# Input transposed by the DMA instead of TensorE, with other activation tables, another parameter layout and another order, in a kernel of windowed attention and a long convolution

## The chip, the cores and the metric

The kernel runs on one core of a Trainium2 chip. The core has TensorE (PE; its weight loads are listed apart as PEld), VectorE (DVE), ScalarE (ACT), GpSimd (POOL) and SyncE (SP), and 16 DMA engines. SP, ACT and POOL issue DMAs from queues of their own, and each engine works through its own instructions in order. The metric is the device time of one execution in microseconds (us).

## The reference

Two branches read the same input `x` of 2048 tokens by 640 channels (bf16), and a gate mixes them. The convolution branch is given `x` as its input, and the separate input `B_u` is not used.

```python
g = sigmoid((x * gate_w).sum(-1, keepdims=True))
# a: attention, 32 heads of 20 channels; token s sees s, s-2, ..., s-14
q, k, v = split(x @ wqkv)
a = (softmax(q . k_window * 20 ** -0.5) . v_window) @ wo
# b: per channel d a kernel of 2048 taps from 192 complex exponentials
dt = exp(log_dt)
K[d, l] = real(sum_n C[d, n] * dt[d] * B[d, n] * exp(dt[d] * A[d, n] * l))
b = irfft(rfft(pad(x)) * rfft(pad(K))) + x * Dskip      # causal convolution
out = g * a + (1 - g) * b
```

`wqkv` is 640 by 1920, `wo` 640 by 640, and each of the six parameter arrays `A_re`, `A_im`, `B_re`, `B_im`, `C_re`, `C_im` is 640 by 192.

## The kernel before, in words

**The work and how it is ordered.** Nearly all work is written as tasks (class `Task`), which are collected in two plans, `"main"` and `"tail"`. A task names the engines that may run it, a planned duration, its dependencies, and at times a due time `rdy` before which a planner did not place it. The table `ORDER` holds, for each plan, the finished sequence: every entry is a step from one task to the next, and a letter behind it chooses the engine of a task that may run on ACT or DVE (the first engine named, ACT, where there is no letter). `emit` writes the instructions in that sequence and ties each instruction to the one before it on its engine, so each engine's order is fixed. What waits for what is settled on the chip by semaphores.

**Start.** `SSMParams.build` issues the loads from three queues. SP loads C_re, C_im, the first quarter of `x`, A_im, the second quarter, the three 640-column parts of `wqkv`, A_re and the other two quarters of `x`. ACT loads B_re, B_im, `log_dt`, `gate_w` and an identity matrix. `x` arrives in the tile `xn` with tokens on the partitions. The projections need channels on the partitions, so `window` (L192) plans ten tasks `turn`, each of eight 128x128 matmuls against the identity (L207) into a PSUM tile `ar`, and ten evictions (`tev`) that copy 128x1024 elements to `xT`, which lies in the buffer `bufA`.

**Projections.** `plan_late` computes q, k and v for four chunks of 512 tokens: 60 tiles `tb` of 128x512, five matmuls each (L291). The 60 evictions go to `pv` (first chunk) or `prj` (the others), by ACT at L473 or DVE at L475, which are the lines of the helper `evict`. From there POOL stores them to DRAM (`qS`, `kS`, `vS`), and `plan_core` reads them back in chunks of 256 tokens (`qc`, `kc`, `vc`). `plan_gate` computes the gate with 80 small matmuls on `xT` (L222).

**Attention.** For each of eight chunks DVE forms products of q with shifted k (`prod`, L345), PE sums them to logits (`lg`, L351), ACT takes the exponential, DVE normalises. SP stores the weights to DRAM (`aS`) and spreads them back (`asb`), DVE multiplies by v (`pv`, L415), PE sums (L422) and projects by `wo` (L446), and ACT or DVE scales by the gate (`ga`).

**Kernel taps.** From the parameters DVE and ACT make ten bf16 tables, called pieces (`pc`): phase digits, log magnitudes, an arctangent for the angle of C times B. That is one long chain of 128x960 instructions with Ln, Exp and Arctan. SP stores each piece into the DRAM table `Sprm` (L620), which has 640 channels, ten pieces and 192 numbers per channel. For each of ten groups of eight channels (`NCH` = 10), `load_L` (L724) loads the rows of that group into one of two tiles `L`. PE multiplies `L` by constants to arguments (`ar`, L767), ACT takes Sin (L782) and Exp (L784) of them into the buffers `big` and `bufA`, DVE multiplies these (`pt` L804, `qq` L806), PE sums over the 192 terms (`kps`, L822). The results `E` of five groups together are expanded (`KExpand`) and written to DRAM.

**Transform.** `first` transforms the taps (`f1`, `fk`) and the input (`fu`) by 128x256 matmuls (L1266; L1285 where a tile is split) with evictions of 128x1024 to `bufA` and `big`. `fft_conv` is the plan `"tail"`: forward transforms (`fp`, L1039) with evictions `sp_u` and `sp_k`, products on DVE (`ta`, `tc`, `Y`), inverse transforms (`cp`, `yp`), the mix with the attention branch (`tt`, `ot`), and the output's stores.

**Activation tables.** [...]

Of the kernel before, what the change touches and what calls it, by code (L numbers as in the profile page):

```python
# [20 lines left out]
S = 2048  # L21
# [17 lines left out]
def _attn_consts():  # L39
# [129 lines left out]
class Attn:  # L169
# [22 lines left out]
    def window(self, pl, cst, pa):  # L192
# [7 lines left out]
        for n in range(2 * NKT):  # L200
# [8 lines left out]
            def ev(en, hf=hf, kt=kt, b=b):  # L209
                evict(nc, en, self.xT[:, hf, kt, :], b["tx"][:].rearrange("p a b -> p (a b)"))  # L210
# [323 lines left out]
class SSMParams:  # L534
# [5 lines left out]
    def build(self, ctx, tc, pl, A_re, A_im, B_re, B_im, C_re, C_im, log_dt, gate_w, at_, pa, xl, wl):  # L540
# [19 lines left out]
        for w_ in wl:  # L560
            w_()
# [803 lines left out]
```

## Time and profile before

| | us |
|---|---|
| runs: median of 3 (lowest to highest) | 342.84 (342.28 to 346.0) |
| profiled execution: span from first to last instruction | 339.6 |
| busy PE / DVE / ACT in that span | 289.5 / 298.9 / 290.2 |
| first projection matmul (L291) starts | 16.44 |
| first Sin (L782) starts | 56.80 |
| first forward transform of the tail (`fp`) starts | 271.65 |

The profiled execution has no device time of its own beside its span. The span of 339.6 is 3.2 us under the median of the timed runs, and I take these 3.2 us as what lies around the span. The profile's rows give the start in us, the duration, the engine, the line, the operation, output and inputs, how often it was repeated (x...), and in brackets how long the engine sat idle and what released it. `SPq`, `ACTq` are the issuing of DMAs by that engine. In tables of stages the columns are the stretch, its length, then busy time and number of instructions of PE, PEld, DVE, ACT and POOL, the granted PE clock (1.00 is full), the mean busy share of the DMA engines and what they moved in GB/s.

### The profile page before, as it was taken

To read this page: it belongs to the slowest core of one execution; us is meant where nothing else is said; L and a number is where in the kernel's file an instruction comes from. 1 tells how busy PE (TensorE), PEld (TensorE's weight loads), DVE (VectorE), ACT (ScalarE), POOL (GpSimd) and SP (SyncE) were. 2 spreads that over 40 slices of the span, in tenths; PEclk is the share of its full clock that TensorE was granted. 3 is DMA by queue.
4 is the path that set the end of the run, shared out by engine and by line. 5 is a ranking of instruction groups with operands and counts; after the bars stand their busy time and mean duration, and the time that the engine had idled before them with its cause. 6 is when DMAs were issued, how large, how long until landed. Compare 5 with 4: busy or idle time off the path is not lost. (4 is left out here: it accounts for less than half of the span.)

```text
span 339.6 us, 12013 instructions
## 1 busy us (share of the span) xinstructions
PE 289.5 (85%) x5181; PEld 172.1 (51%) x5214; DVE 298.9 (88%) x407; ACT 290.2 (85%) x424; POOL 92.3 (27%) x119
## 2 busy tenths in 40 slices
PE   0699999999997899999999979669999899996760
PEld 0446544444453455455545444445765676665750
DVE  3999988789998799999899989786888979999982
ACT  1899737999997899999999998786976779998991
POOL 8603334041052161102137615621130000000053
PEclk9999999999998999999999999997999999999996
DMA  7997854378279781285738585982882336576056
GB/s 251 356 259 233 222 131 133 103 207 166 66 195 249 186 204 38 42 233 161 252 58 206 124 224 129 207 187 50 235 281 93 124 113 198 139 142 118 2 136 177
DMA packets 48949, 56.30 MB, mean 166 GB/s; under 512 B 25498, under 2 KB 40154, under 8 KB 48898
## 3 DMA queue, kind: packets, MB, share of 16 engines
q1 hardware_dynamic: 39928, 27.90, 31.2%
q0 software_dynamic: 8224, 27.04, 30.2%
q8 instruction: 40, 0.66, 0.8%
q10 hardware_dynamic: 746, 0.61, 0.5%
q14 instruction: 11, 0.09, 0.1%
HBM read 36.26 MB, written 19.27 MB: 164 GB/s over the span
## 5 line engine op out<-in xcount | busy, mean ns | idle before, releaser
L291 PE MATMUL tb<-bufA 128*128 128x512 bf16 x267 | 73.3, 389 | 5.0 <-issue 3.1
L782 ACT ACTIVATE big<-ar 128x740 bf16<-128x740 int16 (+1 forms) x72 | 56.1, 854 | 2.5 <-issue 1.2
L784 ACT ACTIVATE big<-ar 128x848 bf16<-128x848 f32 x60 | 50.3, 918 | 1.8 <-PE ar L767 1.8
L767 PE MATMUL ar<-Rarg,L 64*128 64x212 bf16 (+4 forms) x600 | 48.8, 253 | 3.5 <-ACT big L784 1.5
L345 DVE TENSOR_TENSOR prod<-qc,kc 128x2048 bf16<-128x2048 bf16 x40 | 47.8, 1218 | 4.2 <-PE lg L351 3.3
L415 DVE TENSOR_TENSOR pv<-vc,asb 128x2048 bf16<-128x2048 bf16 x40 | 48.2, 1217 | 0.9 <-PE tb L422 0.9
L291 PEld LDWEIGHTS <-bufA 128*128 128x128 bf16 x300 | 31.0, 122 | 28.0 <-issue 11.3
L822 PEld LDWEIGHTS <-pt 128*32 128x32 bf16 (+1 forms) x2560 | 25.8, 92 | 37.0 <-issue 34.4
L822 PE MATMUL kps<-qq,pt 128*32 128x21 bf16 (+1 forms) x2560 | 36.9, 173 | 8.0 <-issue 6.6
L804 DVE TENSOR_TENSOR pt<-big 128x1024 bf16<-128x1024 bf16 x48 | 33.3, 701 | 5.6 <-issue 2.0
L767 PEld LDWEIGHTS <-L 64*128 64x128 bf16 x600 | 20.6, 94 | 27.1 <-issue 23.4
L446 PE MATMUL tb<-wo_sb,oT 128*128 128x320 bf16 x160 | 28.6, 301 | 0.7 <-DVE ga L457 0.4
L1157 POOL DMA_DIRECT2D out_dram<-ot x14 | 7.7, 557 | 77.9 <-DVE ot L1139 77.9
L473 ACT ACTIVATE prj<-tb 128x512 bf16<-128x512 f32 x32 | 20.0, 632 | 8.8 <-PE tb L291 8.6
L422 PE MATMUL tb<-pv,ind 128*64 128x512 bf16 (+1 forms) x192 | 25.0, 363 | 2.5 <-issue 2.3
L473 ACT ACTIVATE sp_u<-fp 128x640 bf16<-128x640 f32 x31 | 23.9, 952 | 0.8 <-PE fp L1039 0.8
L473 ACT ACTIVATE sp_k<-fp 128x640 bf16<-128x640 f32 x29 | 22.6, 969 | 1.2 <-DMA PHX<-c_phi 1.0
L969 POOL COPY pace<-Usb 32x2 bf16<-32x2 bf16 x7 | 14.3, 2045 | 25.9 <-DMA Usb<-in_A_x_dram 25.9
L806 DVE TENSOR_TENSOR qq<-big 128x1344 bf16<-128x1344 bf16 x24 | 21.2, 883 | 0.0
L339 POOL DMA_DIRECT2D vc<-vS x16 | 11.9, 771 | 28.9 <-DVE pv L415 12.4
L1039 PEld LDWEIGHTS <-PHI 128*128 128x128 bf16 x160 | 15.5, 97 | 8.0 <-issue 1.0
L455 ACT ACTIVATE ga<-tb,g_sb 128x320 bf16<-128x320 f32 x26 | 13.8, 544 | 4.4 <-PE tb L446 3.0
(168 smaller groups left out, 562.4 us busy)
## 6 DMA issues: line engine op xcount, KB each, us to landing
vc<-vS POOLq DMA_DIRECT2D x16, 327.5 KB, 6.9
kc<-kS POOLq DMA_DIRECT2D x8, 337.5 KB, 6.1
xn<-in_A_x_dram SPq DMA_DIRECT2D x4, 640.0 KB
qc<-qS POOLq DMA_DIRECT2D x8, 320.0 KB, 5.9
gaS<-ga SPq DMA_DIRECT2D x8, 320.0 KB
Usb<-in_A_x_dram POOLq DMA_DIRECT2D x8, 320.0 KB, 5.1
gaF<-gaS SPq DMA_DIRECT2D x8, 320.0 KB
bufA<-in_A_wqkv_dram SPq DMA_DIRECT2D x3, 800.0 KB
```

The source lines that it names most:

```text
L291: nc.tensor.matmul(ppf, self.wq[:, which, kt, e::5], self.xT[:, c0 // 1024, kt, c0 % 1024:c0 % 1024 + SC], start=(kt == 0), stop=(kt == NK ...
L345: nc.vector.tensor_tensor(b[e][:], b["qc"][:, e, :].unsqueeze(1).to_broadcast([128, W, C]), win(b["kc"][:, e, :], 0, W, DIL, C), ALU.mult)
L415: nc.vector.tensor_tensor(o, vw, b["asb"][:].unsqueeze(2).to_broadcast(sh), ALU.mult)
L422: nc.tensor.matmul(b["op", e][64 * a:64 * a + 64, 0:n, :], ind[:, 32:96], b["pv", e][:, w, a, 0:n, :], start=(w == 0), stop=(w == 3), skip ...
L446: nc.tensor.matmul(apf[:, :320], b["oT"][:, e, i * 128:(i + 1) * 128], wo_sb[:, e, hf * 320:(hf + 1) * 320], start=(e == 0), stop=(e == 4))
L473: nc.scalar.activation(o, i, ACT.Identity)
L767: nc.tensor.matmul(ar[:, g2, a0:a0 + ncol], L[rows, sb, gv, l0:l0 + 128], R[rows, c0:c0 + ncol], start=True, stop=True, tile_position=(64 ...
L782: nc.scalar.activation(d_[:, :, s0 * QW:s1 * QW], ar[:].bitcast(I16)[:, :, 0:2 * (s1 - s0) * QW:2], ACT.Sin, scale=SCL)
L784: nc.scalar.activation(dst[:, gp::2].rearrange("p g s n -> p g (s n)"), ar[:, :, 0:2 * EW], ACT.Exp)
L804: nc.vector.tensor_tensor(pt[:, :, k, :], gg[:, :, ::-1] if k else gg, e1, ALU.mult)
L806: nc.vector.tensor_tensor(qq[:], trg[:, :, KI:].rearrange("p a (v m) -> p a v m", v=2), exq[:, :, KI:].unsqueeze(2).to_broadcast([128, 32, ...
L822: nc.tensor.matmul(kps[32 * g:32 * g + 32, h, NM * ql:NM * ql + NM], pt[rows, k, v, :], qq[rows, k, v, :], start=(g not in started), stop= ...
```

## The change

**Input.** The tile `xn`, the ten `turn` tasks and their ten evictions go. Instead four DMAs of the transposing kind (`dma_start_transpose`, L184 in the new numbering) on SP's queue write a quarter of `x`, 512 tokens by 640 channels, straight into `xT` as 128 channels by 5 by 512 tokens. On that queue the first part of `wqkv` now stands right behind the first quarter of `x`, and the other quarters behind the weights.

**Tables.** At the head of ACT's work the set `natural_log_exp_and_others` is loaded by name, and ahead of the arctangent `trig_and_small`. The compiled kernel has 15 table loads instead of 19.

**Parameter table.** `Sprm` becomes [128, 10, 5, 192]. A piece is stored as 128 runs of 960 numbers (1920 bytes) where it was 640 runs of 192 (384 bytes). A group of eight channels is now made of other channels, one of every five, so that `load_L` needs two DMAs per half instead of four: 40 loads of 160 runs instead of 80 loads of 80 runs, each run 384 bytes as before. What reads or writes by channel follows it: the half that a sum goes to (`kps`), the writing of `E` (elements 5 apart instead of 8 in a row), the columns of `fu`, the layout of `C` and of `Dk`. The load of `wo` waits for the 31st projection tile instead of the last transposition.

**Order.** Both entries of `ORDER` are new. By the compiled instruction lists this moves evictions between the engines: DVE's number of `prj` falls from 13 to 9, of `pv` from 6 to 2 and of `fu`'s evictions to `big` from 6 to 3, and ACT's rises by as many. Ahead of its last piece DVE has two evictions of transpositions and four of `pv` before, and none now. One piece (`pc` from `xl`) moves to ACT, one linear step of the angle to DVE.

```diff
-        xl = [lambda sc=sc: nc.sync.dma_start(xn[:, 4 * sc:4 * sc + 4], xr[:, 4 * sc:4 * sc + 4]) for sc in range(4)]
+        xl = [lambda sc=sc: nc.sync.dma_start_transpose(self.xT[:, sc // 2, :, SC * (sc % 2):SC * (sc % 2) + SC], self.x[SC * sc:SC * sc + SC]) for sc in range(NSC)]
...
-        for n in range(2 * NKT):
...
-            m = pl.add(f"turn{n}", "P", 0.447, turn, acq=["ar"], eq=1024, rdy=(11.3, 23.5)[hf])
-            self.xts.append((m, pl.add(f"tev{n}", "AD", {"A": 0.905, "D": 1.133}, ev, deps=[m], rel=[("ar", m)])))
...
-                    m = pl.add(f"late{n}", "P", 0.432, lambda _, f=mm: f(_, 0, 2), deps=[e_ for m_, e_ in self.xts[5 * (sc // 2):5 * (sc // 2) + 5]], after=[m_ for m_, e_ in self.xts] if sc else [], acq=["tb"], eq=1024, rdy=(13.0, 15.5, 18.0)[which])
+                    m = pl.add(f"late{n}", "P", 0.432, lambda _, f=mm: f(_, 0, 2), acq=["tb"], eq=1024, rdy=max((11.0, 14.0, 16.3)[which], (11.0, 19.0, 22.5, 25.0)[sc]))
...
-        self.S = dr.tile([D, NPC, NST], BF16, name="Sprm")
+        self.S = dr.tile([128, NPC, 5, NST], BF16, name="Sprm")
...
+        nc.scalar.preload_act_table_set("natural_log_exp_and_others")
         load(nc.sync, "cre", C_re); load(nc.scalar, "bre", B_re)
...
         xl[0]()
+        wl[0]()
         load(nc.sync, "aim", A_im)
+        wl[1](); wl[2]()
         xl[1]()
-        for w_ in wl:
-            w_()
         load(nc.sync, "are", A_re)
         xl[2](); xl[3]()
...
-            op(f"sp{i}", "S", 0.36, lambda _: nc.sync.dma_start(Sv[:, :, i, :], t[k][:]), [k], [f"S{i}"], dma=1.1)
+            op(f"sp{i}", "S", 0.36, lambda _: nc.sync.dma_start(self.S[:, i], t[k][:]), [k], [f"S{i}"], dma=1.1)
...
-            act("at", "t1", ACT.Arctan, "atan")
+            def atan(_):
+                SCA.preload_act_table_set("trig_and_small")
+                SCA.activation(t["at"][:], t["t1"][:], ACT.Arctan)
...
-            for v in range(2):
-                for h in range(2):
-                    d0 = 160 * ((2 * v + g + 2 * h) % 4) + 80 * h + 8 * c
-                    src = self.prm.S[d0:d0 + 8].rearrange("(s q) i n -> (q i) s n", q=4)
-                    l0 = NST * (h ^ v)
-                    (self.nc.gpsimd if gs == (1,) else self.nc.sync).dma_start(L[64 * g + 2:64 * g + 2 + 4 * NPC, :, v, l0:l0 + NST], src)
+            for a in range(2):
+                src = self.prm.S.rearrange("(a g x b q) i k n -> a g b k (q i) x n", a=2, g=2, x=4, b=2)[a, g, c // HC, c % HC]
+                (self.nc.gpsimd if gs == (1,) else self.nc.sync).dma_start(L[64 * g + 2:64 * g + 2 + 4 * NPC, :, :, NST * a:NST * a + NST].rearrange("p v s n -> p (v s) n"), src)
...
-        at.wo_in = pl.add("wo", "G", 0.55, at.load_wo, deps=[at.xts[-1][0]], dma=2.1)
-        at.wo_in.waits = [at.xts[-1][0]]
+        at.wo_in = pl.add("wo", "G", 0.55, at.load_wo, deps=late[30:31], dma=2.1)
+        at.wo_in.waits = late[30:31]
```

The next four lists are instruction lists of the compiled kernels, in order, and tell nothing of times. The first is SP's queue at the start before: `cre`, `cim`, `aim`, `are` are parameter arrays, `bufA` holds the weights.

```order
L549 DMA cre<-in_B_C_re_dram 128x960
L549 DMA cim<-in_B_C_im_dram 128x960
L188 DMA xn<-in_A_x_dram 128x4x640
L549 DMA aim<-in_B_A_im_dram 128x960
L188 DMA xn<-in_A_x_dram 128x4x640
L189 DMA bufA<-in_A_wqkv_dram 128x5x640 x3
L549 DMA are<-in_B_A_re_dram 128x960
L188 DMA xn<-in_A_x_dram 128x4x640 x2
L620 DMA Sprm<-pc 640x1x192 x10
```

The same place on SP now:

```order
L531 DMA cre<-in_B_C_re_dram 128x960
L531 DMA cim<-in_B_C_im_dram 128x960
L184 DMA_TRANSPOSE bufA<-in_A_x_dram 128x5x512
L185 DMA bufA<-in_A_wqkv_dram 128x5x640
L531 DMA aim<-in_B_A_im_dram 128x960
L185 DMA bufA<-in_A_wqkv_dram 128x5x640 x2
L184 DMA_TRANSPOSE bufA<-in_A_x_dram 128x5x512
L531 DMA are<-in_B_A_re_dram 128x960
L184 DMA_TRANSPOSE bufA<-in_A_x_dram 128x5x512 x2
L602 DMA Sprm<-pc 128x960 x10
```

The first weights moved ahead of A_im, all weights ahead of the second quarter of `x`. The second place is ACT's start, before (`bre`, `bim` parameters, `ldt` the logarithm of the step, `g` the gate's weights, `ax`, `xl`, `xa` first links of the chain to the pieces; behind these rows the first eviction of a transposition follows):

```order
L549 DMA bre<-in_B_B_re_dram 128x960
L549 DMA bim<-in_B_B_im_dram 128x960
L554 DMA ldt<-in_B_log_dt_dram 128x5
L555 DMA g_115<-in_gate_w_dram 5x128
L259 DMA ident<-c_ident 128x128
L569 ACT_TABLE_LOAD
L569 ACTIVATE dtb<-ldt 128x5
L572 ACTIVATE gw_sb<-ar 128x5
L656 ACT_TABLE_LOAD
L656 ACTIVATE lnd<-dtb 128x5
L599 ACTIVATE xl<-wr 128x960
L599 ACTIVATE ax<-wr 128x960
```

ACT's start now, where `pv<-tb` is the eviction of a projection tile:

```order
L534 ACT_TABLE_LOAD
L531 DMA bre<-in_B_B_re_dram 128x960
L531 DMA bim<-in_B_B_im_dram 128x960
L537 DMA ldt<-in_B_log_dt_dram 128x5
L538 DMA g_114<-in_gate_w_dram 5x128
L241 DMA ident<-c_ident 128x128
L552 ACTIVATE dtb<-ldt 128x5
L555 ACTIVATE gw_sb<-ar 128x5
L581 ACTIVATE ax<-wr 128x960
L581 ACTIVATE xl<-wr 128x960
L455 ACTIVATE pv<-tb 128x512
L581 ACTIVATE xa<-wi 128x960
```

The first table load moved ahead of the DMAs that ACT issues, the second one is gone, and a projection eviction stands where the first transposition's stood. The identity's DMA now also waits for a semaphore that the load of C_re releases. On TensorE, ahead of the first argument matmul (L767 before, L749 now) stand 127 of the 300 projection matmuls, 80 transpositions and 80 gate matmuls before, and 145 projection and 80 gate matmuls now.

More of the change, by code (lines that the diff above doesn't have):

```diff
@@ L178, in __init__, with loads @@
         self.aS = dr.tile([2, 32, W, 256], BF16, name="aS")
-    def loads(self, bufA, xn, cst):
+    def loads(self, bufA, cst):
         nc = self.nc
@@ L198, in window, with plan_gate @@
         nc.gpsimd.dma_start(self.vS[:, :, 0:HALO], zz[:])
[L199 to L214 removed]
+    def plan_gate(self, pl, cst, pa, g_sb):
         nc = self.nc
@@ L245, in store @@
             nc.gpsimd.dma_start(self.omS.rearrange("(i p) -> i p", p=128), b["om2"][:])
[L246 removed]
+        m = pl.add("gate", "P", 2.0, logit, acq=["ar"], eq=80, rdy=25.0)
         e = pl.add("gexp", "A", 0.2, expo, deps=[m], table="exp")
@@ L821, in kmm @@
                                     k = 8 * (2 * (gi % 2) + gi // 2) + ql
-                                    nc.tensor.matmul(kps[32 * g:32 * g + 32, h, NM * ql:NM * ql + NM],
+                                    nc.tensor.matmul(kps[32 * g:32 * g + 32, h ^ (g // 2), NM * ql:NM * ql + NM],
                                                      pt[rows, k, v, :], qq[rows, k, v, :],
@@ L1193, in gated_mix_kernel @@
     pl = Plan("main")
-    xl, wl = at.loads(P["bufA"], P["xn"], acst)
+    xl, wl = at.loads(P["bufA"], acst)
     params = prm.build(c1, tc, pl, B_A_re, B_A_im, B_B_re, B_B_im, B_C_re, B_C_im, B_log_dt, gate_w, at, pa, xl, wl)
     kg = KGen(keep, P["pool"], tc, prm)
-    at.window(pl, acst, pa)
+    at.window(acst)
     Dk = keep.tile([128, 2, CH], BF16, name="Dk")
```

38 lines of the change are left out of this document (15 added, 23 removed), and 96 rows, old and new, of the table ORDER.

## The prediction

> **What bounds the kernel now.** I read the page's busy times first, then a table of four stages, then the timeline at their borders. The stages end where the first projection, the first Sin and the tail begin.
>
> ```profile
> PE 289.5 (85%) x5181; PEld 172.1 (51%) x5214; DVE 298.9 (88%) x407; ACT 290.2 (85%) x424; POOL 92.3 (27%) x119
> ...
> 0.00:16.40 16.40, 4.79 (x41) 4.21 (x42) 10.77 (x14) 8.45 (x11) 12.57 (x17) 1.00 0.93 304
> 16.40:56.80 40.40, 38.73 (x293) 20.85 (x295) 37.22 (x46) 30.65 (x42) 10.24 (x14) 1.00 0.74 207
> 56.80:271.60 214.80, 194.36 (x4022) 108.40 (x4050) 193.37 (x262) 194.59 (x279) 61.75 (x74) 0.98 0.62 159
> 271.60:339.60 68.00, 51.59 (x832) 38.59 (x832) 57.52 (x86) 56.52 (x94) 7.71 (x14) 0.95 0.52 129
> ```
>
> No single engine bounds the whole: PE, DVE and ACT are each busy for 85 to 88%. The first stage is a wait for data (PE works 4.79 of 16.40 us). The second is PE's (38.73 of 40.40). In the long third stage the three are level at 193 to 195 of 214.80, so time falls there only if work goes from all of them, or their idle 20 us shrinks. The tail is the same work before and after.
>
> **The start.** Rows of the timeline at the start and at the first Sin:
>
> ```profile
> 0.74 0.42 ACTq L549 DMA_DIRECT2D bre<-in_B_B_re_dram  x1
> 2.83 0.34 ACTq L259 DMA_DIRECT2D ident<-c_ident  x1
> 3.20 1.28 ACT L569 ACT_TABLE_LOAD   x1 [3.20 <-issue]
> 4.63 1.16 DVE L590 TENSOR_TENSOR wr<-cre,bre 128x960 f32<-128x960 bf16 x1 [3.65 <-DMA bre<-in_B_B_re_dram]
> 8.23 0.16 PE L571 MATMUL ar<-ident,g 5*128 5x5 bf16 x1 [8.23 <-DMA ident<-c_ident]
> 10.90 1.30 PEld L207 LDWEIGHTS <-xn 128*128 128x128 bf16 x13 [2.23 <-DMA xn<-in_A_x_dram]
> 16.44 4.96 PE L291 MATMUL tb<-bufA 128*128 128x512 bf16 x14
> 25.50 2.32 PE L291 MATMUL tb<-bufA 128*128 128x512 bf16 x10
> 55.06 0.53 PE L767 MATMUL ar<-Rarg,L 64*128 64x296 bf16 x8
> 55.50 1.28 ACT L782 ACT_TABLE_LOAD   x1 [0.40 <-PE ar L767]
> ```
>
> At 10.90 the second quarter of `x` has landed: 983 KB of B and C parameters, two quarters of `x` (1311 KB) and A_im (246 KB), 2.54 MB in all. The first projection now needs the same 983 KB, one quarter (655 KB) and one part of the weights (819 KB), 2.46 MB, with A_im landing beside them. If a transposing DMA moves bytes like a plain one, the first projection starts at 11.0 instead of 16.44. The trace has no transposing DMA, so this is bounded: below by about 10.0, from the rates of the first stretches,
>
> ```profile
> 0.00:8.00 8.00, 0.00 (x0) 0.10 (x1) 2.41 (x6) 1.49 (x2) 6.85 (x11) 1.00 0.79 246
> 8.00:12.00 4.00, 1.80 (x16) 1.45 (x16) 3.97 (x5) 3.25 (x5) 3.94 (x5) 1.00 1.06 361
> ```
>
> (246 GB/s for 8 us are 1.97 MB, the remaining 0.49 to 0.74 MB take 1.4 to 2.0 us at 361 GB/s); above by the narrowest transfer of the trace:
>
> ```profile
> vS<-zz POOLq DMA_DIRECT2D x1, 17.5 KB, 7.5
> ```
>
> That one writes 640 separate runs in 7.5 us. A transposed quarter comes to 512 tokens times 5 groups of 128 channels, 2560 pieces; at that pace 30 us, with the start at 32. I take 11.0, by the row at 10.90, since its bytes, queues and moment are the same. [...]
>
> Two things could hold PE longer than `x` does. The identity, which PE's first matmul needs, is now issued when C_re has landed, about 4.6 instead of 2.83; before it landed 5.4 us after its issue (8.23), so now at 10.0, hidden by 1.0 us. The table load ahead of ACT's DMAs delays B_re by 1.28 us, and the parameter chain with it; that is counted below.
>
> From the first projection to the first argument matmul PE needed 55.06 - 16.44 = 38.6 us. Now there stand 145 projection matmuls instead of 127, at 0.232 us (ten in 2.32): 18 x 0.232 = +4.2. The second half's 40 transpositions go:
>
> ```profile
> 16.40:56.80 40.40, 3.13 (x43) 2.57 (x40) 1.00 0.74 207
> ```
>
> -3.1. So 39.7 us, and the first argument at 11.0 + 39.7 = 50.7, 4.4 us earlier than 55.06, with 18 projection matmuls more done. **Term one: -4.4.**
>
> That holds only if `L` is there by then:
>
> ```profile
> 13.51 1.22 DVE L475 CAST bufA<-ar 128x1024 bf16<-128x1024 f32 x1
> 19.41 0.69 DVE L475 CAST pv<-tb 128x512 bf16<-128x512 f32 x1 [0.57 <-PE tb L291]
> 23.84 0.65 DVE L475 CAST pc<-xl 128x960 bf16<-128x960 f32 x1
> 38.50 1.92 DVE L611 TENSOR_SCALAR t<-at 128x960 f32<-128x960 f32 x2
> 41.41 1.14 DVE L627 TENSOR_TENSOR pc<-t,t 128x960 bf16<-128x960 f32 x1
> 47.13 4.66 SPq L732 DMA_DIRECT2D L<-Sprm  x12
> 47.63 2.59 POOL L732 DMA_DIRECT2D L<-Sprm  x4 [6.82 <-issue]
> L<-Sprm POOLq DMA_DIRECT2D x4, 30.0 KB, 2.7
> ```
>
> DVE finished the last piece at 42.55. Ahead of it go two transposition evictions (2 x 1.22), four of `pv` (4 x 0.69) and one cast (0.65), one linear step of 0.96 comes, and the start slips 1.28: 42.55 - 5.85 + 2.24 = 38.9. The piece then took 4.6 us to land (47.13), POOL's issue 2.59 (now half the DMAs, 1.3) and the landing 2.7: `L` at 47.5, hidden by 3.2 us. If the wide runs land faster than 4.6 us, it is hidden by more. The four table loads saved and the eight evictions gone from ACT (7.8 us by the row below) lie in the first two stages, where ACT worked 39 of 57 us: worth nothing by themselves, except that the chain through ACT keeps up with DVE's.
>
> **The middle.** Between first Sin and tail I count evictions from the lists of both kernels:
>
> ```profile
> L473 ACT ACTIVATE bufA<-ar 128x1024 bf16<-128x1024 f32 x8 | 7.8, 1018 | 0.3 <-PE ar L207 0.3
> L473 ACT ACTIVATE big<-bp 128x1024 bf16<-128x1024 f32 x14 | 14.2, 1044 | 2.2 <-PE bp L1266 2.2
> L475 DVE CAST big<-bp 128x1024 bf16<-128x1024 f32 x6 | 7.2, 1221 | 1.7 <-PE bp L1266 1.6
> L473 ACT ACTIVATE prj<-tb 128x512 bf16<-128x512 f32 x32 | 20.0, 632 | 8.8 <-PE tb L291 8.6
> L475 DVE CAST prj<-tb 128x512 bf16<-128x512 f32 x13 | 8.9, 686 | 3.5 <-PE tb L291 3.5
> ```
>
> ACT gets three of `big` and two of `prj`: 3 x 1.044 + 2 x 0.632 = +4.4. DVE loses three of `big` and four of `prj`: 3 x 1.221 + 4 x 0.686 = -6.4. PE has the 18 matmuls behind it, -4.2. Other swaps come to under 1 us on each. Since the three were level, I spread the sum over them: (4.4 - 6.4 - 4.2) / 3 = -2.1. Its bounds are +4.4, if ACT alone sets the pace, and -6.4, if DVE alone did. [...] Fewer `L` issues on SP cost nothing and hide nothing that the waits show. **Term two: -2.1. The tail: 0.**
>
> **Sum.** 339.6 - 4.4 - 2.1 = 333.1 for the profiled span; with the 3.2 us around it, the median goes from 342.84 to 336.3. Cross-check: the removed work is 7.8 us of PE, 7.8 of ACT, 2.4 of DVE and four loads (5.1), 23.1 in all; spread over three level engines it is 7.7.
>
> **Rivals.** *ACT becomes the bound of the middle.* For it:
>
> ```profile
> 100.00:120.00 20.00, 16.88 (x393) 8.19 (x396) 16.27 (x20) 16.17 (x24) 4.04 (x5) 0.91 0.90 210
> 120.00:190.00 70.00, 66.20 (x1591) 35.02 (x1601) 68.08 (x97) 69.70 (x106) 25.33 (x27) 1.00 0.55 145
> 190.00:240.00 50.00, 41.01 (x1065) 24.16 (x1064) 42.40 (x63) 42.22 (x63) 16.84 (x22) 0.97 0.72 162
> 240.00:271.60 31.60, 29.00 (x221) 20.99 (x220) 27.95 (x31) 24.11 (x34) 3.84 (x7) 1.00 0.55 183
> ```
>
> ACT has 0.3 us free in 120 to 190. Against it: the three big evictions fall after 240, where 7.5 us are free. Then +4.4 eats the -4.4: 342.8. Chance 0.18.
>
> *The idle stretches shrink.* In 100 to 120 and 190 to 240, where DMAs are busiest, ACT idles 3.8 and 7.8 us and
>
> ```profile
> PE kps L822 <- issue: 6.6, 6, 2.0
> ```
>
> PE stalls up to 2.0 us on nothing but its own issue. If fewer and wider DMAs halve these 11.6 us, 5.8 more are gained: 330.5. Against it: the heavy loads of attention stay. Chance 0.15.
>
> *Slower: the transposing DMA moves in small pieces.* The first quarter then blocks SP's queue with the weights behind it. At the pace of `zz` the start is at 32 instead of 11.0, +21, and the forecast's 336.3 becomes 357. It decides from a start at 17.5, where the gain of 6.5 is gone; it is slower by over 1% from 21. For it speaks only that row, against it every wide load here. [...] Chance 0.11.
>
> **How the numbers follow.** The forecast keeps 0.56, with a range of 332 to 340 of its own. 1% of 342.84 is 3.4 us, about what a measurement of this kernel can tell from no change. Faster by more (under 339.4): 0.50 of the forecast, all of the idle rival, 0.03 of ACT's, 0.68. Within: 0.06 + 0.15, 0.21. Slower: 0.11. The range from 329.5, the idle rival's end and a little, to 344.0, ACT's, leaves out the slow transposition and some of the upper gain.
>
> **What would show it.** First projection at 10 to 12 and transposing DMAs of 2 to 4 us each on a queue that isn't held up; first argument matmul near 50.7, waited for by nothing of `L`; 15 table loads of 1.28; the middle near 212.7 with ACT's busy time up by 4 and DVE's down by 6; the tail at 68. Wrong: a first projection after 15, an argument waiting for `L`, ACT without idle time in a middle of 217 or more, or a tail that moves by over 2 us.

## The result, and the profile after

The changed kernel takes 352.69 us (median of 4 runs, 352.1 to 355.56), the kernel before 342.56 beside it: a ratio of 1.0386 with a 95% interval of 1.0316 to 1.0455. It is 3.9% slower; 336.3 was forecast. The profiled execution has a span of 350.3 us, 10.7 more than before. Ratios compare the executions in the fast state and so need not equal the quotient of the medians, which are over all executions.

The table of stages after; the stages end at the first projection, at 30.0 us, at the last piece, at the first Sin and at the start of the tail:

```profile
0.00:12.50 12.50, 0.16 (x1) 0.10 (x1) 6.92 (x10) 3.45 (x5) 11.29 (x16) 1.00 0.89 234
12.50:30.00 17.50, 17.42 (x82) 8.49 (x84) 11.27 (x12) 11.63 (x19) 2.92 (x5) 1.00 1.10 276
30.00:46.50 16.50, 11.22 (x104) 6.08 (x102) 12.73 (x14) 6.96 (x10) 2.16 (x2) 0.79 0.58 194
46.50:60.40 13.90, 13.44 (x85) 6.38 (x86) 9.94 (x17) 7.52 (x12) 4.53 (x6) 1.00 0.53 160
60.40:280.50 220.10, 189.88 (x4017) 110.97 (x4035) 190.88 (x256) 203.70 (x286) 52.33 (x77) 0.95 0.62 158
280.50:350.30 69.80, 52.00 (x832) 38.63 (x831) 58.22 (x87) 56.14 (x93) 7.70 (x14) 0.94 0.52 119
```

The start, the middle and the tail are all longer than before: the first Sin comes 3.65 us later (60.45 instead of 56.80), the middle takes 220.1 instead of 214.8, the tail 69.8 instead of 68.0. In the third row TensorE works 11.2 of 16.5 us at a granted clock of 0.79. Before, it was busy for 12.64 us from 30.0 to 43.7:

```profile
30.00:43.70 13.70, 12.64 (x145) 8.17 (x146) 13.39 (x16) 10.78 (x15) 4.31 (x5) 1.00 0.79 223
```

SP's queue in the timeline after (start, length of the issue):

```profile
1.67 5.30 SPq L184 DMA_TRANSPOSE bufA<-in_A_x_dram  x1
...
9.73 9.04 SPq L184 DMA_TRANSPOSE bufA<-in_A_x_dram  x1
18.82 0.58 SPq L531 DMA_DIRECT2D are<-in_B_A_re_dram  x1
19.44 7.75 SPq L184 DMA_TRANSPOSE bufA<-in_A_x_dram  x2
27.31 19.42 SPq L602 DMA_DIRECT2D Sprm<-pc  x10
48.48 2.33 SPq L714 DMA_DIRECT2D L<-Sprm  x6
```

The transposing DMAs hold SP's queue: 3.9 us each where two stand together (7.75 / 2), 5.3 for the first and 9.0 for the second, for which the profile names no releaser. The load of A_re between them holds it for 0.58. The first store of a piece runs at 27.31; before, it ran at 18.87:

```profile
18.87 24.22 SPq L620 DMA_DIRECT2D Sprm<-pc  x10
```

What that sets off, engine by engine:

```profile
30.78 0.66 DVE L457 CAST pc<-xa 128x960 bf16<-128x960 f32 x1 [2.98 <-DMA Sprm<-pc]
34.25 1.16 DVE L609 TENSOR_TENSOR pc<-xa,pc 128x960 bf16<-128x960 f32 x1 [2.81 <-DMA Sprm<-pc]
35.33 1.15 DVE L572 TENSOR_TENSOR t<-wi,t 128x960 f32<-128x960 f32 x1
36.51 1.00 ACT L648 ACTIVATE at<-t 128x960 f32<-128x960 f32 x1 [5.40 <-DVE t L572]
37.42 0.58 ACT L455 ACTIVATE pv<-tb 128x512 bf16<-128x512 f32 x1
38.05 11.75 PE L273 MATMUL tb<-bufA 128*128 128x512 bf16 x45 [5.23 <-ACT pv L455]
45.23 1.15 DVE L609 TENSOR_TENSOR pc<-xl,pc 128x960 bf16<-128x960 f32 x1
58.72 0.53 PE L749 MATMUL ar<-Rarg,L 64*128 64x296 bf16 x8
```

VectorE fills its four buffers for pieces (the pool `sp_pc` has four) and waits twice for a store. Behind it ScalarE's arctan waits, behind the arctan an eviction of a projection, and behind that TensorE for 5.23 us. The last piece is done at 46.4 (45.23 + 1.15; before 42.55), and the first argument matmul runs at 58.72 (before 55.06, forecast 50.7).

In the middle one stop stands out. TensorE stops within a group of `kps`, "issue" being nothing that the profile shows, and ScalarE waits for it:

```profile
88.73 0.37 PE L804 MATMUL kps<-qq,pt 128*32 128x21 bf16 x31
91.83 0.18 PE L804 MATMUL kps<-qq,pt 128*32 128x21 bf16 x1 [2.73 <-issue]
92.04 1.13 ACT L455 ACTIVATE E<-kps 128x336 bf16<-128x336 f32 x1 [2.18 <-PE kps L804]
```

The 10 us from there on in the table of stretches:

```profile
90.00:100.00 10.00, 6.97 (x47) 2.57 (x49) 7.89 (x9) 6.66 (x9) 0.85 (x1) 0.50 0.24 74
```

TensorE's granted clock is 0.50 in all of them. And the eviction behind the stop takes 1.13 us, where the same shape took 0.45 before.

### The profile page after: what moved, and what is told of

Its sections match the earlier page's. It is cut to its first block, busy times and chain, and to the rows that moved or that the text cites. A ratio compares the mean times of both kernels' runs of the same rounds, so it can differ in the third digit from the quotient of the medians.

```text
span 350.3 us, 11749 instructions
## 1 busy us (share of the span) xinstructions
PE 284.1 (81%) x5112; PEld 170.7 (49%) x5134; DVE 290.0 (83%) x394; ACT 289.4 (83%) x423; POOL 80.9 (23%) x117
## 3 DMA queue, kind: packets, MB, share of 16 engines
q0 software_dynamic: 8192, 27.04, 30.2%
## 5 line engine op out<-in xcount | busy, mean ns | idle before, releaser
L273 PE MATMUL tb<-bufA 128*128 128x512 bf16 x278 | 76.9, 409 | 11.1 <-ACT pv L455 5.2
L749 PE MATMUL ar<-Rarg,L 64*128 64x212 bf16 (+4 forms) x600 | 49.7, 260 | 15.6 <-ACT big L764 6.5
L273 PEld LDWEIGHTS <-bufA 128*128 128x128 bf16 x300 | 32.8, 123 | 44.7 <-issue 22.9
L766 ACT ACTIVATE big<-ar 128x848 bf16<-128x848 f32 x60 | 50.7, 911 | 2.3 <-PE ar L749 2.3
L749 PEld LDWEIGHTS <-L 64*128 64x128 bf16 x600 | 23.1, 96 | 47.2 <-issue 44.7
L804 PE MATMUL kps<-qq,pt 128*32 128x21 bf16 (+1 forms) x2560 | 27.4, 176 | 5.3 <-issue 3.9
L804 PEld LDWEIGHTS <-pt 128*32 128x32 bf16 (+1 forms) x2560 | 23.6, 92 | 12.5 <-issue 10.5
L455 ACT ACTIVATE prj<-tb 128x512 bf16<-128x512 f32 x36 | 21.9, 619 | 6.6 <-PE tb L273 6.5
L455 ACT ACTIVATE sp_u<-fp 128x640 bf16<-128x640 f32 x31 | 22.4, 875 | 1.3 <-PE fp L1020 1.3
L404 PE MATMUL tb<-pv,ind 128*64 128x512 bf16 (+1 forms) x192 | 23.1, 360 | 0.3 <-DVE pv L397 0.3
L455 ACT ACTIVATE sp_k<-fp 128x640 bf16<-128x640 f32 x28 | 20.4, 874 | 1.2 <-PE fp L1020 1.2
L428 PEld LDWEIGHTS <-oT 128*128 128x128 bf16 x160 | 14.8, 99 | 9.6 <-issue 4.3
L455 ACT ACTIVATE big<-bp 128x1024 bf16<-128x1024 f32 x17 | 17.1, 1030 | 0.9 <-PE bp L1251 0.5
```

The lines of the kernel that those rows point to most:

```text
L273: nc.tensor.matmul(ppf, self.wq[:, which, kt, e::5], self.xT[:, c0 // 1024, kt, c0 % 1024:c0 % 1024 + SC], start=(kt == 0), stop=(kt == NK ...
L404: nc.tensor.matmul(b["op", e][64 * a:64 * a + 64, 0:n, :], ind[:, 32:96], b["pv", e][:, w, a, 0:n, :], start=(w == 0), stop=(w == 3), skip ...
L428: nc.tensor.matmul(apf[:, :320], b["oT"][:, e, i * 128:(i + 1) * 128], wo_sb[:, e, hf * 320:(hf + 1) * 320], start=(e == 0), stop=(e == 4))
L455: nc.scalar.activation(o, i, ACT.Identity)
L749: nc.tensor.matmul(ar[:, g2, a0:a0 + ncol], L[rows, gv, sb, l0:l0 + 128], R[rows, c0:c0 + ncol], start=True, stop=True, tile_position=(64 ...
L766: nc.scalar.activation(dst[:, gp::2].rearrange("p g s n -> p g (s n)"), ar[:, :, 0:2 * EW], ACT.Exp)
```

## The experiments

Two suspects come out of this first, the transposing DMAs on SP's queue (theory Q) and the newly searched order (theory O); later the evictions into `E` and the fetch of instructions join them. All runs in one table; "first argument" and "span" are of the profiled execution, and each ratio is against the kernel before, run beside it:

| run | median us | ratio (95%) | first argument | span |
|---|---|---|---|---|
| changed kernel | 352.69 | 1.0386 (1.0316 to 1.0455) | 58.7 | 350.3 |
| plain_loads | 341.96 | 1.0035 (0.9986 to 1.0085) | 49.1 | 341.2 |
| order_of_before | 345.66 | 1.0140 (1.0014 to 1.0265) | 56.3 | 345.2 |
| stores_on_pool | 352.25 | 1.0379 (1.0271 to 1.0486) | 56.8 | 345.4 |
| plain_order_of_before | 347.29 | 1.0107 (1.0020 to 1.0194) | 54.6 | 339.8 |
| plain_order_of_before_2 | 344.32 | 1.0132 (1.0067 to 1.0196) | 55.5 | 340.9 |
| hold_alone | 359.34 | 1.0514 (1.0403 to 1.0625) | 65.7 | 356.2 |
| tables_and_runs_alone | 344.10 | 1.0101 (1.0055 to 1.0147) | 54.9 | 341.4 |
| tables_and_runs_dense_E | 340.75 | 0.9962 (0.9900 to 1.0024) | 54.8 | 334.0 |
| dense_E | 350.37 | 1.0267 (1.0208 to 1.0326) | 59.3 | 346.3 |
| plain_dense_E | 340.27 | 0.9999 (0.9958 to 1.0040) | 49.0 | 336.5 |
| fetch_88_on | 366.57 | 1.0776 (1.0699 to 1.0852) | 59.5 | 364.0 |
| fetch_240_on | 357.35 | 1.0479 (1.0423 to 1.0536) | 61.8 | 352.0 |
| before_88_on | 344.25 | 1.0079 (1.0023 to 1.0134) | 55.1 | 342.8 |
| fetch_88_wo_early | 360.85 | 1.0550 (1.0474 to 1.0625) | 60.0 | 357.8 |

Executions of one kernel lie up to 2 to 3% apart here, so a single span is good for the place of an event and not for a verdict; verdicts go by the ratios.

### Plain loads

```diff
-nc.sync.dma_start_transpose(self.xT[...], self.x[SC * sc:SC * sc + SC])
+nc.sync.dma_start(self.xT[...], self.x[SC * sc:SC * sc + SC].rearrange("(p j) d -> p (j d)", j=4))
```

> The changed kernel with its four transposing DMAs replaced by plain DMAs of the same bytes on the same queue (the transposition is left out; all other instructions and their order stay). Theory Q (queue): the transposing DMAs hold SP's queue until 27.3 us, the ten stores of pieces stand behind them, DVE stops on its four piece buffers, and this is where the loss comes from. Then the first store of a piece starts before 21 us, DVE waits for no store, the first argument matmul runs at 50 to 52 us instead of 58.7, and the time falls by at least 7 us, to 341 to 346 us. Theory O (order): the newly searched order loses the time itself in the middle. Then the start becomes earlier as well, but from the first Sin to the tail it still takes 219 to 222 us (before: 214.8), and the time stays at 346 us or above.

```profile
10.89 3.52 SPq L184 DMA_DIRECT2D bufA<-in_A_x_dram  x2
16.66 22.11 SPq L602 DMA_DIRECT2D Sprm<-pc  x10
...
47.28 1.92 PE L273 MATMUL tb<-bufA 128*128 128x512 bf16 x8
49.13 0.53 PE L749 MATMUL ar<-Rarg,L 64*128 64x296 bf16 x8
```

341.96 us, 10.7 less. The first store runs at 16.66, VectorE waits for no store, the first projection starts at 10.84 (forecast 11.0) and the first argument at 49.13 (forecast 50.7). Theory Q holds for the start. But the middle of this execution, from the first Sin at 50.9 to the tail at 270.5, still takes 219.6 us, as theory O said (the 346 us or more that it gave did not come): with the whole start as forecast, the kernel is only as fast as before. It is a probe and no usable kernel, since `x` is not transposed.

### The order of before, and plain loads in it

The 20 tasks of the transposition on TensorE are taken out of the order string of before, and the rest is used in the changed kernel:

```diff
-ORDER = {...}   # newly searched
+ORDER = {...}   # of before, without turn0..9 and tev0..9
```

> The changed kernel (transposing DMAs, tables named, wide parameter table) with the order and the engine choices of the kernel before, the 20 tasks of the transposition on TensorE left out. Theory Q: the stores of pieces still stand behind the transposing DMAs, so that the first argument matmul is at 57 us or later and the time is 346 to 352 us. Theory O: the new order is what costs; in the old one the middle takes 213 to 216 us and the tail 68 us, and the time is 340 to 345 us whatever the start does.

345.66 us, just outside both: theory Q had 346 us or more and the first argument at 57 or later (it is at 56.3), theory O had 340 to 345 with a middle of 213 to 216 (it is 217.9). Neither fits alone, and with an interval of 1.0014 to 1.0265 from four executions the comparison with the kernel before is unclear. The run with plain loads in that order completes the square.

> The changed kernel with plain loads in place of the transposing DMAs (the transposition is left out) and with the order of the kernel before: the fourth cell beside the changed kernel (352.7), plain loads (342.0) and the order of before (345.7). Theory O (the new order costs the middle whatever the loads do): 334 to 338 us, with a middle of 213 to 216 us. Rival: the new order is neutral and only meets the transposing DMAs badly; then 341 to 344 us.

> The plain loads in the order of before once more, since four executions from 341.5 to 348.5 us don't tell it from plain loads in the new order (342.0). If the new order is the better one for early data, it stays 2 to 5 us above plain loads in the new order, at 344 to 347 us; if the orders are equal, it is 341 to 343 us.

The two runs have 1.0107 and 1.0132, and medians of 347.29 and 344.32. Theory O's 334 to 338 us is refuted, though the middle that it named came (214.0 and 214.1). The rival's 341 to 344, the new order being neutral, was passed too; the second run lies where it was expected if the new order is the better one for early data. In the old order plain loads show no gain over transposing ones (1.0140, within its wide interval); in the new order they gain 3.5% (1.0386 to 1.0035). So neither the transposing DMAs nor the order loses the 3.9% alone; the two together do. By the profiles, the new order with plain loads has its first argument 5.5 to 6.4 us earlier than the old order with them (49.1 for 54.6 and 55.5), and gives that back in the middle (219.6 for 214.0 and 214.1). The 1.0 to 1.4% that the three runs in the old order stay behind the kernel before is about what two parts of the change cost by themselves, as shown further down (1.0101).

The waits of VectorE in the old order with transposing DMAs say why the stores do no harm there; the four longest from 4 to 60 us (total, times, longest):

```profile
DVE wr L574 <- DMA bre<-in_B_B_re_dram: 3.7, 1, 3.7
DVE prod L329 <- PE lg L335: 1.7, 2, 1.4
DVE dtc L628 <- ACT dtb L554: 1.4, 1, 1.4
DVE tau L574 <- DMA aim<-in_B_A_im_dram: 1.2, 1, 1.2
```

There the stores start at 26.7 us too, but VectorE doesn't wait for one: that order has its fourth piece done at 27.0 and begins the fifth at 29.6. In the new order the fourth is done at 22.4, and VectorE stands before the fifth from 27.8; the arctan and the evictions come behind it.

### Stores on GpSimd, and the hold alone

```diff
-op(f"sp{i}", "S", 0.36, lambda _: nc.sync.dma_start(self.S[:, i], t[k][:]), ...)
+op(f"sp{i}", "G", 0.36, lambda _: nc.gpsimd.dma_start(self.S[:, i], t[k][:]), ...)
```

> The changed kernel with the ten stores of pieces issued by GpSimd instead of SP, so that they no longer stand behind the transposing DMAs. Theory Q: DVE's waits of 2.98 and 2.81 us for a piece's store go, the arctan starts 4 to 6 us earlier than at 36.5, TensorE doesn't stop for 5.2 us at 33, the first argument matmul comes at 51 to 54 us, and the time falls to 343 to 347 us. Theory O: the start gains the same, but the middle stays at 219 to 222 us, and the time at 347 us or above.

A miss in the time (theory Q had 343 to 347 us) and half a miss in the start. The arctan runs at 29.74 instead of 36.51 and the last piece is done at 41.4, but another wait takes the place of the one removed:

```profile
33.66 0.69 PE L204 MATMUL ar<-gw_sb,bufA 128*128 128x1 bf16 x20 [3.84 <-DMA bufA<-in_A_x_dram]
34.21 11.97 PE L273 MATMUL tb<-bufA 128*128 128x512 bf16 x42
```

TensorE now stops for the last quarter of `x`, and the first argument comes at 56.8. The four executions run from 347.2 to 354.4 us, and what the change of queue gains is unclear (the profiled execution was the fastest of them, so its 345.4 says little). To tell the held queue from the late quarters, hold_alone loads the quarters plainly and holds SP behind them with four transposing DMAs that nobody reads:

```diff
 xl[2](); xl[3]()
+dump = pin.tile([128, 5, 256], BF16, name="dump")
+for sc in range(NSC):
+    nc.sync.dma_start_transpose(dump[:], at_.x[256 * sc:256 * sc + 256])
```

> The changed kernel with plain loads in place of the transposing ones, as in plain loads (the transposition is left out), and behind the last load four transposing DMAs of 256 tokens each into one scratch buffer that nobody reads, ahead of the first store of a piece on SP's queue: the data of x come as early as with plain loads, but the stores of pieces are held up. Theory H (the held stores are what costs in the start): the first store runs at 27 us or later, VectorE waits for a piece's store again, the first argument matmul comes at 55 to 58 us, and the time is 347 to 352 us. Theory L (the late landing of the transposed quarters costs, as the 3.84 us pause for x in the run with the stores on GpSimd says): the first argument matmul stays at 49 to 52 us, and the time at 341 to 344 us.

SP's queue in the timeline:

```profile
14.52 22.72 SPq L549 DMA_TRANSPOSE dump<-in_A_x_dram  x4
37.33 16.01 SPq L606 DMA_DIRECT2D Sprm<-pc  x10
```

The waits from 4 to 62 us (total, times, longest):

```profile
DVE pc L457 <- DMA Sprm<-pc: 14.6, 1, 14.6
ACT at L652 <- DVE t L576: 14.3, 1, 14.3
PE tb L273 <- ACT pv L455: 14.1, 1, 14.1
```

359.34 us, above the range of both theories, because the hold lasted to 37.33 instead of some 27: 5.7 us for each of the four (22.72 / 4), where two of the changed kernel took 3.9 each. That each also waits for the one before it, for the same buffer, is my reading of the code; no row shows it. It is the changed kernel's chain of three waits, each 14 us long, with the data of `x` there in time. So held stores set off the chain by themselves. What they would cost with a hold to 27.31 this run does not say, since its hold is 10 us longer. The late last quarter is a second limit: it shows when the stores are gone from SP's queue, and also, with the stores on it, in three of the runs below (waits of 1.7 to 4.4 us).

### Two parts alone, and the evictions into E

The kernel before with the named tables and the wide parameter table, all else as it was:

> The kernel before with two parts of the change alone: the table sets named and the parameter table in wide runs with its channels per chunk; the loads, the transposition on TensorE and the order are those before. By the prediction's terms: one table load of 1.28 us less before the first activations and shorter loads of L, with nothing given back: the first argument matmul 1 to 3 us earlier than 55.06, the middle 214 to 215 us, the time 338 to 341 us. Rival: the scattered writes of E and the strided columns in the middle cost more than that gives, with a middle of 217 us or more, and the time at 342 to 345 us.

344.10 us, 1.0% slower than before: the rival's time, though with a middle of 215.9 and not of 217. The start is where it was (first argument 54.9 for 55.06): the earlier table load and the wide stores give nothing there. The groups of evictions into `E`, before and then here:

```profile
L473 ACT ACTIVATE E<-kps 128x336 bf16<-128x336 f32 x6 | 2.7, 453 | 1.9 <-PE kps L822 1.9
L475 DVE CAST E<-kps 128x336 bf16<-128x336 f32 x4 | 2.0, 503 | 1.8 <-PE kps L822 1.8
```

```profile
L473 ACT ACTIVATE E<-kps 128x336 bf16<-128x336 f32 x6 | 6.8, 1128 | 1.3 <-PE kps L822 1.3
L475 DVE CAST E<-kps 128x336 bf16<-128x336 f32 x4 | 4.4, 1088 | 0.0
```

Writing single elements at steps of five instead of runs of eight made the same eviction 2.2 to 2.5 times as long (1088 ns for 503, 1128 for 453). The cure keeps the wide table: the channels of a tile stand in the order chunk, position, and the later matmuls pick their columns to match.

```diff
-half["E"][:].rearrange("p m (c q k) -> p c m q k", c=2, k=HC)[:, :, :, :, cl]
+half["E"][:].rearrange("p m (c k q) -> p c m k q", c=2, k=HC)[:, :, :, cl]
-col = sf[:, 4 * n + ql::40]
+col = sf[:, (4 * n + ql) % 5 * 8 + (4 * n + ql) // 5::40]
```

(the split columns and the addition of the skip weights likewise).

> The kernel before with the named tables and the wide parameter table, and E written in runs of eight. Theory E: the slow evictions were the whole loss of 3.4 us of these two parts, and the time is that of the kernel before, 339.5 to 342 us. Rival: the strided columns or the shorter loads of L cost by themselves, and it stays at 343 to 345 us.

> The changed kernel with E written in runs of eight neighbours again (channels of a tile in the order chunk, position instead of position, chunk; the columns that the later matmuls read are picked to match, so the result is the same). In the trace of the two parts alone an eviction into E takes 1.13 us on ScalarE and 1.09 on VectorE, before 0.45 and 0.50. Theory E: this is a loss of the change itself, in a middle where ScalarE has hardly any idle time: the ten evictions are back at 0.45 to 0.50 us, about 6.5 us of busy time less on the two engines, and the time falls by 2.5 to 5 us, to 347.5 to 350.5 us. Rival N: the evictions are hidden, the middle is set by the order and by the instruction fetch, and the time stays within 1 us of 352.7.

> The changed kernel with both steps undone that the runs so far name: plain loads (the transposition is left out) and E in runs of eight. If the two are independent, the gains of 10.7 and 3 to 4 us add up, and the time is 337 to 339.5 us, near the 336.3 that was forecast. If the eviction only mattered behind the late start, it stays at 341 to 343 us.

```profile
L455 ACT ACTIVATE E<-kps 128x336 bf16<-128x336 f32 x8 | 3.9, 492 | 2.3 <-PE kps L804 2.3
L457 DVE CAST E<-kps 128x336 bf16<-128x336 f32 x2 | 1.0, 502 | 0.0
```

These are the evictions of dense_E. With the two parts alone the ratio falls from 1.0101 to 0.9962, 4.7 us of 342, and the loss of these parts is gone; in the changed kernel from 1.0386 to 1.0267, 4.1 us by the ratios, whose intervals just touch, and 2.3 by the medians (its 350.37 is at the upper end of what was expected). With plain loads it is 1.2 us by the ratios (1.0035 to 0.9999), whose intervals overlap; the 340.27 us lie between the ranges for gains that add up and for gains that don't. Both cures together bring the new order to the time of before, and not to 336.3. No version that still transposes beat the kernel before by more than the measurement can tell.

Why ScalarE's time counts, TensorE's waits in the middle tell. Its waits for the Sin of the arguments (total, times, longest), before and then in the changed kernel:

```profile
PE ar L767 <- ACT big L782: 1.3, 3, 0.7
```

```profile
PE ar L749 <- ACT big L764: 6.5, 14, 1.4
```

All its waits of over 0.15 us for ScalarE there sum to 3.8 us before and 19.2 in the changed kernel. They are 18.7 in plain_loads, 15.2 in dense_E and 14.0 in plain_dense_E, and 5.0 to 5.4 in the three runs that put the order of before into the changed kernel. So in the new order, by these traces, ScalarE sets the pace of the middle; no run moves its evictions back by themselves. It is busy there for 203.7 of 220.1 us in the changed kernel, 203.6 of 219.6 in plain_loads, 198.4 of 214.5 in dense_E and 198.2 of 215.9 in plain_dense_E. Single executions scatter around that: stores_on_pool has 202.4 of 215.7 with the slow evictions.

### The fetch of instructions

The page after has a queue for instructions:

```profile
PE 284.1 (81%) x5112; PEld 170.7 (49%) x5134; DVE 290.0 (83%) x394; ACT 289.4 (83%) x423; POOL 80.9 (23%) x117
...
q8 instruction: 40, 0.66, 0.8%
```

0.66 MB for TensorE's 10246 matmuls and weight loads are 64 bytes each, and 40 transfers of 16.4 KB are 256 instructions each. No two of these transfers land less than 3.34 us apart in the changed kernel, and 3.38 in the kernel before. In the 16 profiled executions I looked for stretches in the middle in which TensorE ran nothing for 1.5 us or more, counted the number of the instruction behind each in TensorE's rows of the trace, and took the remainder by 256. (Two traces lack some records, 22 in the changed kernel's and 33 in that before; these are counted in. The numbers that the expectations name are 14 to 19 higher.) All 29 stand at a remainder of 193; some of them:

```
kernel before     107.7 us  no. 2497     221.4 us  no. 7617     228.7 us  no. 7873
changed kernel     91.8 us  no. 1473
before_88_on      106.9 us  no. 2497     207.1 us  no. 6849
fetch_88_on       121.7 us  no. 2753     161.7 us  no. 4289     186.2 us  no. 5057
fetch_240_on       95.3 us  no. 1729     122.5 us  no. 2753
order_of_before   206.6 us  no. 6593     225.1 us  no. 7361
plain_dense_E      82.4 us  no. 1473
```

And in all 29 TensorE goes on 1.3 to 1.7 us after a transfer of the instruction queue has landed (in the changed kernel it lands at 90.5, and TensorE goes on at 91.8). So TensorE stops there for its next block. If that is right, shifting the program by instructions that cost nothing moves the stops to other work:

```diff
 nc.tensor.matmul(lt[:, 0, 0:5], g5[:], at_.ident[0:5, 0:5], start=True, stop=True)
+for _ in range(44):   # 120 in the second run
+    nc.tensor.matmul(lt[:, 1, 0:5], g5[:], at_.ident[0:5, 0:5], start=True, stop=True)
```

> The changed kernel with 44 more tiny matmuls (88 instructions with their weight loads) that write an unused PSUM bank at 8.4 us, where TensorE waits for the first weights anyway; nothing else is changed. In the traces so far every pause of TensorE without a releaser over 0.9 us in the middle stands before an instruction whose number in TensorE's program is 207 to 212 past a multiple of 256. Theory F (fetch): instructions come in blocks of 256 (the 40 transfers of 16 KB on the instruction queue), a pause comes where 256 instructions are used up in less time than the next block takes. By the changed kernel's trace, 88 instructions on, the spans between block borders would be short of 3.3 us by 11.1 us in all, instead of 1.65: the pauses move to other numbers of the code, the one of 2.7 us at 89 us is replaced by four to six others, and the time rises by 4 to 12 us, to 356 to 365 us. Rival N: the place of the borders doesn't matter, and the time stays at 350 to 355 us.

> The same with 120 tiny matmuls (240 instructions). Theory F: the spans between block borders would be short of 3.3 us by 0.39 us instead of 1.65, the pause of 2.7 us at 89 us and the half clock behind it go, and the time falls by 2 to 6 us, to 346 to 351 us, if the added matmuls don't delay the first projection. Rival N: 350 to 355 us.

> The kernel before with the same 44 tiny matmuls (88 instructions) at its first matmul of the gate weights, as a control to the run that shifted the changed kernel by 88 and rose to 366.6 us. Theory F: in the order of before no 256 instructions are used up in less than 3.5 us wherever the borders lie, so that it hardly feels them: 339 to 344 us, and no pause of TensorE without a releaser over 2.5 us in the middle. Rival (the tiny matmuls themselves cost, or any shift does): at least 5 us above before, 346 us or more.

The added matmuls run while TensorE waits for weights, and the first projection starts no later; then the longest stop of fetch_88_on:

```profile
9.44 1.31 PE L556 MATMUL ar<-ident,g 5*128 5x5 bf16 x44
12.48 1.90 PE L273 MATMUL tb<-bufA 128*128 128x512 bf16 x4 [1.73 <-DMA bufA<-in_A_wqkv_dram]
...
121.70 1.87 PE L273 MATMUL tb<-bufA 128*128 128x512 bf16 x4 [6.77 <-issue]
```

366.57 us, 14 more from 44 matmuls of 1.31 us in all: theory F, above its own range. fetch_240_on was to gain and lost 4.7 us; its stop at 95 us is shorter (2.1 us), but one of 6.1 us came at 122. Its profiled execution, the fastest of the four, loses 3.1 us ahead of the first argument, where TensorE waits 4.15 us for the last quarter of `x`, and its middle is 2.2 us shorter than the changed kernel's (217.8 for 220.1). That the stops lie at block borders holds; how long they are doesn't follow from the span between borders alone, as I had assumed. The control says that the sensitivity is the changed kernel's: the same shift adds 0.8% to the kernel before (1.0079) and 3.9% to the changed one (1.0386 to 1.0776). Its 344.25 us is just above the expected 339 to 344, and it has one stop of 2.9 us where none over 2.5 was expected.

How long the stop of 6.77 us is depends on what the DMA engines have to do there, as the last run shows. The transfers of fetch_88_on from 110 to 121 us (share of 16 engines last):

```profile
q0 software_dynamic: 586, 2.25, 101.1%
q8 instruction: 1, 0.02, 0.8%
```

GpSimd's loads fill all 16 engines, and the one block of instructions of these 11 us starts at 118.8. The last run moves 800 KB out of that burst:

```diff
-at.wo_in = pl.add("wo", "G", 0.55, at.load_wo, deps=late[30:31], dma=2.1)
-at.wo_in.waits = late[30:31]
+at.wo_in = pl.add("wo", "G", 0.55, at.load_wo, dma=2.1)   # in the order behind "consts", 74 us
```

> The changed kernel with 88 more instructions on TensorE, as in the run of 366.6 us, and the load of the output weights (800 KB, two DMAs of GpSimd at 108 us) moved to 74 us, between the constants of the convolution. Theory B (a block of instructions waits behind GpSimd's burst of transfers): with a quarter of the burst of 105 to 116 us gone, the pause of 6.77 us at 121.7 us falls to 4 us or less, and the time by 2 to 6 us, to 360 to 364 us. Rival: the pause has another cause and stays at 6 to 7 us, and the time at 365 to 368 us.

```profile
118.94 1.02 PE L274 MATMUL tb<-bufA 128*128 128x512 bf16 x4 [1.01 <-issue]
```

The same block border costs 1.01 us instead of 6.77, and the time falls by 5.7 us to 360.85: theory B. A new stop of 2.6 us stands at 86.8; the moved load is issued at 75.2.

## Why the prediction was wrong, step by step

- **First projection at 11.0, from bytes:** the bytes were right and the mechanism wrong. With plain loads it starts at 10.84; with transposing DMAs at 12.52. Quarter by quarter, a transposing DMA's 2560 packets of 256 bytes take 3.5, 3.5, 2.9 and 4.0 us (the first from 5.0 to 8.5; 655 KB in 3.5 us are 187 GB/s, beside other transfers). They lie within the 2 to 4 us that were named for one, an estimate that no run of before shows, and far from the 30 at the pace of `zz`.
- **The table load delays B_re by 1.28 us:** wrong, and without consequence. ACT issues B_re at 0.78 us, beside its table load at 0.75. The identity was no limit either, as forecast.
- **`L` hidden by 3.2 us, last piece at 38.9: the step that failed in the start.** It was summed over VectorE's work alone. The stores of pieces stand on the same SP queue as the transposing DMAs, and I had followed that queue only to the weights. The rival "small pieces" looked at the right queue and at the wrong transfers: it priced a late first projection (decided from 17.5), and the first projection was at 12.52. The stores were held to 27.31, VectorE had no fifth buffer, and arctan, eviction and TensorE followed. The first argument slipped by 8.0 us against the forecast (58.7 for 50.7). With the hold and the late quarters gone it is at 49.1, so term one (TensorE's 39.7 us from 11.0) was right to 1.4 us: 49.13 - 10.84 = 38.3.
- **TensorE paid for the pause twice.** After the 5.23 us it works at half the clock until 41.9, and the 0.79 in the row of 30 to 46.5 is that. I had no term for it. Of the 9.6 us between the first arguments of the changed kernel and plain_loads, 1.7 are the first projection, 5.2 the pause and about 1.9, as an estimate, the half clock from 38.05 to 41.9 (half of 3.8).
- **`E`'s scattered writing at nothing: the step that failed in the middle.** The forecast has no term for it, and no run shows that it costs nothing. An eviction into `E` took 2.2 to 2.5 times as long: ScalarE's eight cost 9.1 us in all instead of 3.6 (8 x 0.453), in a middle where ScalarE is busy for 203.7 of 220.1. Of the 7.4 us that the middle is longer than forecast (220.1 for 212.7), that is about 4 by the ratios of dense_E; the middles of the two profiled pairs differ by 5.5 and 3.8, and with plain loads the ratios show only 1.2.
- **ACT +4.4, DVE -6.4, spread to -2.1: mis-sized too.** The moved evictions came, but ScalarE's busy time rose by 9.1 (203.70 for 194.59), since `E` came on top, and VectorE's fell by 2.5 only (190.88 for 193.37): its evictions to `prj` and `big` fell by 7.8 us, but products and evictions to `oT` that had stood elsewhere came into the middle, the swaps that were put at under 1 us. With `E` in runs ScalarE has 198.4, near the count (194.59 + 4.4), and the middle takes 214.5 to 215.9 instead of 212.7. So the mean over three level engines gave a gain of 2.1 where the fullest of them got more work and the others waited for it (TensorE for 19.2 us): the rival "ACT becomes the bound" had the right mechanism and deserved more than its 0.18.
- **The idle stretches shrink (0.15):** only ScalarE's did, from 20.2 us of the middle to 16.4, and it had more work in them; TensorE's grew from 20.4 to 30.2, most of it waiting for ScalarE. The row "PE kps <- issue" on which the rival rested is TensorE at its block borders, and it fell from 6.6 us to 3.9. What grew is the longest of these stops (2.73 us for 2.0) and the half clock: 20.5 us of the middle, where it was 6.8. The new order packs `kps` so closely that a block is used up in 2.6 us (86.5 to 89.1), where in the complete traces of the order of before none takes less than 3.5 from border to border. What the stops and the half clock cost in the changed kernel was not isolated.
- **Tail unchanged:** 69.8 for 68.0, on the border of what I called wrong, and 69.9 to 70.7 in the runs with plain loads in the new order. Not taken apart.

In sum, the forecast span was 333.1 and the span is 350.3. Of the 17.2 between them 8.0 are the start, 7.4 the middle and 1.8 the tail. Undoing the two failed steps gives a median of 340.27, the time of the kernel before and 4 us above the forecast (the profiled execution, with a span of 336.5, is the second fastest of twelve). What is left of the middle, 2 to 3 us, is as large as the gain of 2.1 that the mean had claimed; no run isolates it from the half clock.

## What to carry to other kernels

Follow every queue that a slow issue stands on to its end, and for each transfer behind it ask how many buffers its producer has before it stops: here ten small stores mattered more than the weights. A layout made for a DMA was paid for here where an engine writes it (0.45 us became 1.13): look at the innermost step of each eviction that it changes. Spread a sum of work over level engines only if none of them gets more of it: here the one that did, ScalarE, was busy for 203.7 of 220.1 us and TensorE waited for it for 19.2. And when an order packs many tiny matmuls together, count the instructions: 20 of the 29 stops came behind a block of 256 that was used up in 1.3 to 3.6 us (the others behind 4.2 to 6.0), and 23 of the 29 had half the clock granted within 3.5 us of their end.

## What the runs showed of the hardware that I had not expected

- A transposing DMA of 512 tokens by 640 channels held the issuing queue for 3.9 us (7.75 for two), a plain DMA of the same bytes for 0.6 to 1.8 (3.52 for two).
- TensorE's instructions come in blocks of 256 (40 transfers of 16.4 KB, 0.8% of the 16 DMA engines' time in the changed kernel). A block that came amid 2.25 MB of GpSimd's transfers made TensorE wait for 6.77 us; 44 matmuls that take 1.31 us, and move the borders, cost 14 us.
- The granted clock fell to 0.50 at 89.7 us, 0.6 us after TensorE had stopped, and came back at 103.3, though TensorE was at work again from 91.8. The half clock lasted 13.7 us there, and 6.8 us in the start, from 35.05 to 41.88. In the 3.40 us ahead of 89.7 TensorE was busy for 2.35:

```profile
86.30:89.70 3.40, 2.35 (x143) 1.59 (x140) 3.01 (x4) 3.40 (x6) 0.00 (x0) 0.99 1.00 198
```

What sets the granted clock no run here shows.
